# Batch 0's keys in five whole pieces, fewer dummy products, and a new order of every queue

## The chip, the cores and the metric
One core of a Trainium2 chip runs the whole program. It has TensorE (PE, matrix products), VectorE (DVE), ScalarE (ACT), GpSimd (POOL) and SyncE (SP, which only issues transfers), each with a queue of its own that it works through in order. The metric is the time on the device in microseconds (us); lower is better.

## The reference, cut to what matters
Three stages in float32 follow one another: attention over 2 batches, 8 heads, 768 positions and 64 values a head; a gated network with two weight matrices of 512x1024 and a gate of 512x512; and a mixer over positions and channels.

```python
k_sum = k.reshape(B, H, nb, 32, D).max(axis=3)          # block maxima of the keys
v_sum = v.reshape(B, H, nb, 32, D).mean(axis=3)
scores_l = where(|i - j| < 16, scale * q @ k.T, -1e9)    # a window of near keys
scores_s = scale * q @ k_sum.T + log(32)                # and all 24 block maxima
x = softmax(concat(scores_l, scores_s)) @ concat(v, v_sum)
x = sigmoid(xr @ w_r) * (relu(xk @ w_k) ** 2 @ w_v)      # xk, xr: x mixed with its row before
u = x + (relu(x.T @ w_tok1) @ w_tok2).T
out = u + relu(u @ w_ch1) @ w_ch2
```

The weights come as float64 and are turned on the chip into two float32 parts, so each weight product is made of three.

## The kernel before, in words
A batch's queries are cut into 6 tiles of 128 positions. For a tile, the key tile `kw` holds 160 keys (the window) and, in front and behind, 24 columns for the block maxima. Every score row needs the maxima of all blocks, so no score can be made before all of the batch's keys have been seen. For batch 0 `k_load` (L484) brings six key tiles of 128x4x160 by SP and ScalarE's queue in turn, `k_max` (L489) takes the maxima of a tile on VectorE into `ks`, and `kw_sums` (L497) copies `ks` into the two places of a tile on GpSimd.

For one tile and one of the two heads of a pair ("unit"; 12 in batch 0) `s_stage` (L563) makes scores on TensorE (`sp<-kw,xT`), VectorE adds the mask and takes the row minimum of the negated score (`pe`, `mn`), ScalarE takes the exponential and its sum (`pe`, `dens`). TensorE transposes (`pt`), the result is copied (`PT`), and TensorE multiplies it with values (`pv`). `rb` spreads one over the sums over the array, and VectorE multiplies it in (`xT<-xT,rb`). `vt_sum` (L512) adds up v's blocks on VectorE (`vrs`), two rows of 768 elements in one instruction, and `vp` transposes these sums. `q_load` (L555) brings q of batch 0 into a part of `xT` that is free then.

As soon as two tiles of x are there, the weight products of the second stage start: `ko` (with w_k, in groups of two blocks of 128 columns) and `acc` (with w_v). A weight tile (`wst`, 512 KB) is turned into two parts by ScalarE, VectorE, ScalarE (`w<-wf`) and GpSimd in turn. The products are laid between the attention's.

Dummy products, `spin` (L826), whose result nothing reads, run on TensorE: eight of 512 columns at the start, one more of that width after each of the first eight units' scores, and `paced` (L833): one of 256 columns for each key tile but the first, which reads `ks` and so comes behind that tile's maxima.

The order on every engine is written out by hand in `PLANS` (L57), a list of tile names with counts; `keep` (L231) ties each instruction to the one before it in the list. So an engine never works ahead of an instruction that waits. SP's list is the order in which transfers are issued; at most eight of them are on the way at a time.

Of the kernel before, what the change touches and what calls it, by code (L numbers as in the profile page):

```python
# [14 lines left out]
ALU = mybir.AluOpType  # L15
# [16 lines left out]
SPIN0, PACED = 8, 1  # L32
# [26 lines left out]
        spin*12 sp*16 spin sp*24 spin pt*4 sp*8 spin vp pt vp spin pt vp*2 pt*2 spin pt*4 sp*8 rb*8 pt spin pt  # L59
        pv*16 pt sp*8 pt spin pv*16 pt*4 rb*8 sp*8 pt*2 pt@24 pt@22*2 pt@25*2 pv*16 pt sp*8 rb*8 sp*16 pt*4 pv*8  # L60
        pt*3 pv*8 pt spin rb*8 ko pt*2 ko*7 pt@40 ko*3 pt@38 ko*10 pt@41 ko*3 spin ko*2 pt@39 ko*2 pt@42 ko pt
        ko pv*8 rb*8 ko*2 pv*8 acc ko*10 pv*8 acc ko*3 acc ko*3 vp*2 sp*16 acc ko*2 pt ko*2 pt*2 acc ko pt ko
        acc*4 acc@12 acc@9*2 ko*2 vp pv*8 acc rb*8 ko*5 acc@13 acc@15 ko*3 acc*2 ko*4 acc@21 acc@14 ko*4 acc@18
        ko*2 acc acc@22 vp acc@20 sp*16 ko*3 acc@24 ko acc@23 ko*2 acc@27*3 ko acc@33 acc@25*2 sp*16 acc@30 ko
        pt acc pt ko acc acc@34 pt ko*3 acc ko*4 pt*2 ko*3 pt ko pt@56 pt@54 sp ko pt ko pt@57 sp*15 pt pv*16 pt
        ko*3 pt ko*17 pt ko*2 pt ko acc pt acc ko pt*3 acc@39 pv*16 ko pt acc ko acc@38 ko acc@42 ko acc@41
        acc@43 ko acc ko*4 pt acc*3 ko*7 acc pt ko*4 acc ko acc@51*2 pt ko acc@50 ko pt ko acc@54*2 acc@53
        acc@57 ko*9 acc@56 ko*2 pv*16 ko*5 acc@58 ko acc ko acc*2 acc@63 pt ko*2 acc ko*3 acc@62 ko pt sp*3
        acc@66 acc@65 acc@67 pt*2 acc ko*10 acc@72 ko*2 pt ko*8 pt acc@69*2 ko*2 acc acc@73 ko*2 acc acc@78
        acc@75*3 ko acc@81 pt ko acc acc@79 ko*9 acc@83 pt acc@87 ko*8 pv*16 ko acc@80 acc@88*2 acc@84 ko*4  # L70
# [12 lines left out]
        ro*2 acc ro@21 ko ro acc@211 ko ro acc@215 ko*2 acc@212 ko acc@219 ko*10 acc@216*2 ko acc@220 ko*6 ro ko
        acc@218 ro acc@221*2 ro ko acc@225 ro@36*3 ro@27 acc*2 ro@39*3 ro@28 ro@42 ro@29 acc@223*2 ro ro@43
        acc@231 ro@31*4 acc@228 ro@44 ro@35 acc ro@45*2 ko*2 ro ko*7 acc ko*8 acc@234 acc@232*2 ko*7 ro acc@237
        ro@60 acc acc@235 ko*2 acc@239 ko*3 ro@49 ko ro acc@236 ro*3 ko ro*3 ko ro ro@61 h1 ko ro ro@58 ko*3 ro
        ko*7 acc@240 ko*5 ro@63 acc*2 acc@246 ro acc@243*3 ko*5 ro acc@247 acc@249*2 acc@248 acc@251 acc@255
        ro*4 ko*3 ro ko ro ko*6 acc@252 acc@256 ko*2 ro acc@253 ko acc@257 ko h1 ko*5 ro*2 acc@254 acc@258*2
        ro*2 ko*3 acc ro acc*2 ko*4 ro*3 ko ro ko h1 ro ko*7 h1@18 ko ro@84 ko*3 h1@3 acc ko ro ko*2 ro acc@267
        h1 ro acc@264 acc@268*2 acc@265 ro ko acc ro@83 acc@273 ro@89*2 h1@19 acc@270 ro*3 acc@274 h1 acc@271 ro  # L90
        h1@5*2 ro h1*2 acc@275 h1 acc@272 acc@276*2 h1 acc@279 h1 acc acc@278 acc@282 acc@281 acc@283 h1 acc@285
        h1 acc h1@21*2 acc@284 acc@287 h1@14 ro h1 ro@108 h1*2 ro@97*2 ro@109 h1@23*2 ro@99 ro@110 h1*2 ho@12
        ro@100*2 h1*2 ro@111 ro@102 h1 ro*4 ro@112*3 h1*6 ho*2 ro@107 ro@115*2 ho*2 ro*3 ho*2 ho@21 ho@19 ho@22
        ho@20 ro ho@23 ro@132 ro@121 ro@133 ro@122*4 ro@134*4 ro@126*2 ro@138*4 h1 ro*2 h1*2 ro@128*4 h1*8
# [1270 lines left out]
```

## Time and profile before

| | |
|---|---|
| time, median of 3 runs | 494.56 us (493.72 to 495.25) |
| the profiled execution's own time | 495.46 us |
| its span, first to last instruction | 493.7 us |
| TensorE busy | 482.9 us (98%), 3290 products |
| VectorE busy | 293.4 us (59%) |
| ScalarE busy | 248.1 us (50%) |
| GpSimd busy | 210.3 us (43%) |
| transfers | 70.63 MB, mean 143 GB/s |

Busy time of TensorE counts each product to the end of its pipeline, so a busy TensorE can still have small waits between products, and dummy products count as busy. A product in plain float32 stands in the trace as two products. An engine's share over the whole span says little here: VectorE is busy for 59% of the span, and much more than that in the first 64 us. The granted clock in the rows (PEclk) is a share of full speed.

### The profile page before, as it was taken

How to read it: one execution, taken by the hardware profiler on the slowest of the kernel's cores; microseconds unless marked ns; L12 is line 12 of the kernel's file. 1: busy time of each engine (PE TensorE's matmuls, PEld its weight loads, DVE VectorE, ACT ScalarE, POOL GpSimd, SP SyncE). 2: the span in 40 equal slices, each digit the busy share in tenths (PEclk: the TensorE clock that was granted, in tenths of full speed). 3: DMA queues.
4: the chain of work that ended last, by engine and by line, in shares of the span. 5: the costliest groups of instructions: out<-in, count | busy, mean ns of one | idle time of the engine just before them, and what ended most of it. 6: DMA issues, size and time to landing. Idle time of an engine off the chain costs nothing.

```text
span 493.7 us, 8740 instructions
## 1 busy us (share of the span) xinstructions
PE 482.9 (98%) x3290; PEld 403.3 (82%) x3290; DVE 293.4 (59%) x638; ACT 248.1 (50%) x569; POOL 210.3 (43%) x266
## 2 busy tenths in 40 slices
PE   8999999999999999999999999999999999999996
PEld 3678787888898888888888767787898888988884
DVE  3699996544543243757777788268395537354253
ACT  1698758763545663575876542554543323111110
POOL 5246577864545224263455333858815501100000
PEclk9999999999999999999999999999999999999998
DMA  9999961340200520002646746828860405061402
GB/s 271 336 319 345 339 206 21 118 134 21 61 1 2 193 105 1 0 1 53 208 158 224 253 102 214 293 83 250 271 241 20 149 27 187 18 219 42 150 1 85
DMA packets 35914, 70.63 MB, mean 143 GB/s; under 512 B 3072, under 2 KB 12288, under 8 KB 35872
## 3 DMA queue, kind: packets, MB, share of 16 engines
q1 hardware_dynamic: 34288, 69.09, 43.7%
q10 hardware_dynamic: 1584, 0.98, 0.6%
q8 instruction: 26, 0.43, 0.4%
q14 instruction: 16, 0.13, 0.1%
HBM read 60.04 MB, written 9.44 MB: 141 GB/s over the span
## 4 chain that ended last, share of the span: by engine, by line
PE 84%; DVE 7%; issue 3%; POOL 3%; ACT 2%; DMA 1%; DVEq 0%; POOLq 0%; SPq 0%; ACTq 0%
PE o L225 16%; PE ko L225 14%; PE acc L225 14%; PE m L225 9%; PE ro L225 7%; PE go L225 5%; PE spin L225 4%; PE sp L225 3%; PE pv L225 3%; PE h L225 3%; PE pt L225 2%; DVE wf L225 2%; POOL w L225 2%; PE ho L225 1%; DVE ybuf L225 1%
## 5 line engine op out<-in xcount | busy, mean ns | idle before, releaser
L225 PE MATMUL o<-w,gh 128*128 128x512 f32 x288 | 100.7, 399 | 0.3 <-ACT gh L225 0.2
L225 POOL TENSOR_TENSOR w<-wf,w 128x512 fp32r<-128x512 f32 x50 | 69.6, 1399 | 53.9 <-ACT w L225 53.7
L225 PE MATMUL m<-u,w 128*128 128x256 f32 x504 | 85.7, 282 | 0.9 <-ACT f L225 0.7
L225 PE MATMUL ko<-xh,w 128*128 128x256 f32 x384 | 84.8, 288 | 0.6 <-ACT rl L225 0.5
L225 PEld LDWEIGHTS m<-u,w 128*128 128x128 f32 x504 | 77.4, 189 | 8.9 <-ACT f L225 1.2
L225 PEld LDWEIGHTS ko<-xh,w 128*128 128x128 f32 x384 | 65.2, 188 | 7.5 <-ACT rl L225 1.3
L225 PE MATMUL acc<-w,kh 128*128 128x512 f32 x192 | 68.4, 403 | 0.0
L225 PEld LDWEIGHTS o<-w,gh 128*128 128x128 f32 x288 | 52.3, 188 | 9.3 <-ACT gh L225 1.7
L225 POOL TENSOR_TENSOR kl<-rl,kh 128x512 fp32r<-128x512 f32 x24 | 31.5, 1314 | 58.7 <-ACT kh L225 42.5
L225 PE MATMUL o<-w,gl 128*128 128x512 f32 x144 | 54.7, 395 | 0.0
L225 PE MATMUL ko<-xl,w 128*128 128x256 f32 x192 | 54.6, 285 | 0.0
L225 PE MATMUL go<-u,w 128*128 128x512 f32 x144 | 45.4, 400 | 0.1
L225 ACT ACTIVATE wst<-wst 128x512 f32<-128x512 f32 x62 | 40.2, 670 | 8.5 <-DMA wst<-in_moe_w_ch_dram 8.5
L225 ACT ACTIVATE pe<-pe,mn 128x120 f32<-128x120 f32 x96 | 37.0, 387 | 14.7 <-DVE mn L225 14.1
L225 DVE SCALAR_TENSOR_TENSOR xk<-xT,mus,tmp 128x256 f32<-128x256 f32 x52 | 31.0, 613 | 16.0 <-ACT tmp L225 12.4
L225 ACT CAST w<-wf 128x512 fp32r<-128x512 f32 x50 | 30.4, 616 | 19.8 <-DVE wf L225 17.5
L225 ACT ACTIVATE gh<-m 128x512 fp32r<-128x512 f32 x24 | 14.2, 598 | 51.2 <-DVE m L225 51.2
L225 DVE SCALAR_TENSOR_TENSOR wf<-wst,wf 128x512 int32<-128x512 int32 x50 | 36.5, 735 | 3.6 <-ACT wst L225 2.5
L225 PEld LDWEIGHTS acc<-w,kh 128*128 128x128 f32 x192 | 34.2, 188 | 5.1 <-issue 0.5
L225 PEld LDWEIGHTS ko<-xl,w 128*128 128x128 f32 x192 | 36.1, 188 | 2.4 <-issue 0.2
L225 PE MATMUL acc<-w,kl 128*128 128x512 f32 x96 | 37.8, 400 | 0.0
L225 DVE TENSOR_SCALAR wf<-wst 128x512 int32<-128x512 int32 x50 | 28.2, 568 | 15.2 <-POOL w L225 15.2
(111 smaller groups left out, 897.5 us busy)
## 6 DMA issues: line engine op xcount, KB each, us to landing
wst<-in_moe_w_ch_dram SPq DMA_DIRECT2D x36, 512.0 KB
w<-stored SPq DMA_DIRECT2D x24, 512.0 KB
stored<-w SPq DMA_DIRECT2D x24, 256.0 KB
wst<-in_moe_w_k_dram SPq DMA_DIRECT2D x8, 512.0 KB
wst<-in_moe_w_v_dram SPq DMA_DIRECT2D x8, 512.0 KB
wst<-in_moe_w_tok_dram SPq DMA_DIRECT2D x6, 512.0 KB
out_dram<-o SPq DMA_DIRECT2D x12, 256.0 KB
kw<-in_k_dram SPq DMA_DIRECT2D x9, 320.0 KB
```

Of the source, the lines that this page charges most:

```text
L225: inst = fn(*args, **kw)
```

## The change
Batch 0's keys come as a tensor of their own, `ka`, laid out by pair of heads, in pieces of 128x800 (the last cut into 416 and 384 columns), on SP alone. They land in `kall`, the end of `ybuf`, which later holds values and results. The maxima are taken from there, a piece at a time, and each key tile is copied on the chip from `kall`: tiles 0 to 3 on ScalarE (tile 0 in two halves), tiles 4 and 5 on GpSimd. q of batch 0 is stored so that each row of it is one stretch in `xT`. v's sums of batch 0 are four instructions instead of two. ScalarE gets a first exponential of one column, so that its table is loaded at once. The paced products are gone; six dummies of 512 columns stand at the start, and the units' dummies have 256. All five lists in `PLANS` are new, from start to end.

```diff
-SPIN0, PACED = 8, 1
+SPIN0 = 6
+KA = 4
@@ PLANS: all five lists
...
+    warm = const.tile([128, 1], F32, name="warm")
+    nc.scalar.activation(warm, ident[:, 0:1], AF.Exp)
...
     def k_load(b, t):
-        q = nc.scalar if b == 0 and t % 2 else nc.sync
-        after(q.dma_start(kw[:, :, K0:K0 + 2 * HALF], k[b, t]))
+        after(nc.sync.dma_start(kw[:, :, K0:K0 + 2 * HALF], k[b - 1, t]))
+    NKA = NP * (S + 2 * WINDOW)
+    kall = ybuf.rearrange("p a n -> p (a n)")[:, B * NT * DM - NKA:].rearrange("p (a s) -> p a s", a=NP)
+    def halves(p):
+        return ((0, S // 2), (S // 2, S)) if p == NP - 1 else ((0, S),)
+    def keys_load(p):
+        for i, j in halves(p):
+            i, j = i and i + 2 * WINDOW, j + 2 * WINDOW
+            nc.sync.dma_start(kall[:, p, i:j], ka[p][:, i:j])
+    def keys_max(p):
+        for i, j in halves(p):
+            x = kall[:, p, WINDOW + i:WINDOW + j].rearrange("p (n w) -> p n w", w=BLOCK)
+            nc.vector.tensor_reduce(st_of(0)["ks"][:, p, i // BLOCK:j // BLOCK], x, AX.X, ALU.max)
+    def keys_copy(t):
+        kw = st_of(0)["kw"][t] = at.tile([128, NP, WC], F32, tag="kw", bufs=KB, name="kw")
+        for ps in (slice(0, 2), slice(2, NP)) if t == 0 else (slice(0, NP),):
+            dst, src = kw[:, ps, K0:K0 + 2 * HALF], kall[:, ps, 128 * t:128 * t + 2 * HALF]
+            if t < KA:
+                nc.scalar.copy(dst, src)
+            else:
+                nc.gpsimd.tensor_scalar(dst, src, 1.0, 1.0, ALU.mult, ALU.mult)
...
     def vt_sum(b, j):
-        r = nc.vector.tensor_reduce(st["vr"][:, 2 * j:2 * j + 2], st.pop(("vt", j)), AX.X, ALU.add)
-        if b == 0:
-            behind(r, lows[-1:])
+        x = st.pop(("vt", j))
+        for c in range(2) if b == 0 else (slice(0, 2),):
+            r = nc.vector.tensor_reduce(st["vr"][:, 2 * j:2 * j + 2][:, c], x[:, c], AX.X, ALU.add)
...
     def attention():
-                    spin(SPIN)
+                    spin(SPIN, 2)
...
-    def spin(n):
+    def spin(n, w=4):
...
-            after(nc.tensor.matmul(o, ident, ident.unsqueeze(1).to_broadcast([128, 4, 128]), start=True, stop=True))
-    def paced(t):
...
+            after(nc.tensor.matmul(o[:, :w], ident, ident.unsqueeze(1).to_broadcast([128, w, 128]), start=True, stop=True))
     spin(SPIN0)
+    for p in range(NP):
+        keys_load(p)
+    for p in range(NP):
+        keys_max(p)
     for t in range(NT):
-        k_load(0, t)
+        keys_copy(t)
```

TensorE's list at its start, before: the first dummies, the paced products (`spin<-ks`), the first scores.

```order
L225 MATMUL spin<-ident 128x512 x8
L225 MATMUL spin<-ks,ident 128x256 x4
L225 MATMUL sp<-kw,xT 64x120 x16
L225 MATMUL spin<-ks,ident 128x256
L225 MATMUL sp<-kw,xT 64x120 x24
L225 MATMUL spin<-ident 128x512
L225 MATMUL pt<-ident,pe 120x128 x4
L225 MATMUL sp<-kw,xT 64x120 x8
```

The same place after the change:

```order
L235 MATMUL spin<-ident 128x512 x6
L235 MATMUL spin<-ident 128x256 x2
L235 MATMUL sp<-kw,xT 64x120 x16
L235 MATMUL spin<-ident 128x256
L235 MATMUL pt<-ident,pe 120x128
L235 MATMUL sp<-kw,xT 64x120 x16
L235 MATMUL spin<-ident 128x256 x2
L235 MATMUL vp<-ident,vrs 24x128
L235 MATMUL pt<-ident,pe 120x128 x3
L235 MATMUL vp<-ident,vrs 24x128 x3
L235 MATMUL sp<-kw,xT 64x120 x16
```

No product reads `ks` any more; two of the units' dummies stand ahead of the first score, and the transposes of v's sums come earlier among the scores.

SP's list at its start, before (`xT<-in_q` and `xT<-in_vt` are q and v for the sums, `wst` the weights, `ybuf<-in_v` the values):

```order
L225 DMA kw<-in_k_dram 128x4x160 x3
L225 DMA xT<-in_q_dram 128x4x128 x3
L225 DMA xT<-in_vt_dram 128x2x768 x2
L225 DMA ybuf<-in_v_dram 96x512
L225 DMA wst<-in_moe_w_k_dram 128x512
L225 DMA wst<-in_moe_w_v_dram 128x512
L225 DMA xT<-in_q_dram 128x4x128
```

And after:

```order
L235 DMA ybuf<-in_ka_dram 128x800 x3
L235 DMA ybuf<-in_ka_dram 128x416
L235 DMA ybuf<-in_ka_dram 128x384
L235 DMA xT<-in_q_dram 128x512 x2
L235 DMA mus<-in_mu_dram 128x8
L235 DMA xT<-in_vt_dram 128x2x768 x2
L235 DMA wst<-in_moe_w_v_dram 128x512
L235 DMA xT<-in_q_dram 128x512
L235 DMA ybuf<-in_v_dram 96x512
```

The five pieces of keys stand first, then two tiles of q; the other three key tiles that ScalarE's queue issued are gone from there.

SP's list further on, before: from the third w_k tile (`wst_147`) to batch 1's key tiles (`kw`).

```order
L225 DMA wst_147<-in_moe_w_k_dram 128x512
L225 DMA wst_155<-in_moe_w_v_dram 128x512
L225 DMA wst_149<-in_moe_w_v_dram 128x512
L225 DMA wst_153<-in_moe_w_k_dram 128x512
L225 DMA kw_625<-in_k_dram 128x4x160
L225 DMA wst_157<-in_moe_w_k_dram 128x512
L225 DMA ybuf_71<-in_v_dram 96x512
L225 DMA kw_810<-in_k_dram 128x4x160
L225 DMA wst_161<-in_moe_w_k_dram 128x512
```

And after, from batch 1's first key tile to the sixth w_k tile (`wst_170`):

```order
L235 DMA kw_461<-in_k_dram 128x4x160
L235 DMA kw_624<-in_k_dram 128x4x160
L235 DMA wst_166<-in_moe_w_k_dram 128x512
L235 DMA kw_809<-in_k_dram 128x4x160
L235 DMA ybuf_73<-in_v_dram 96x512
L235 DMA kw_1013<-in_k_dram 128x4x160
L235 DMA kw_1121<-in_k_dram 128x4x160
L235 DMA wst_168<-in_moe_w_v_dram 128x512
L235 DMA kw_1123<-in_k_dram 128x4x160
L235 DMA ybuf_73<-in_vt_dram 128x1536
L235 DMA qT_922<-in_q_dram 128x512
L235 DMA wst_170<-in_moe_w_k_dram 128x512
```

All six key tiles of batch 1 and its first v for the sums now stand ahead of the sixth w_k tile.

## Rows read from the trace of the kernel before

**Rows 1.** Busy us (count) by stage, all engines; then clock, transfer share, GB/s

```profile
14.00:36.00 22.00, 21.26 (x245) 15.29 (x245) 19.04 (x85) 18.37 (x75) 6.79 (x14) 1.00 1.07 318
36.00:50.00 14.00, 14.00 (x188) 11.24 (x188) 12.73 (x48) 12.48 (x35) 8.63 (x8) 1.00 1.05 347
50.00:64.00 14.00, 13.26 (x133) 11.26 (x130) 12.98 (x27) 10.28 (x30) 9.02 (x9) 1.00 1.06 353
...
120.00:200.00 80.00, 80.00 (x617) 70.39 (x616) 32.54 (x85) 42.10 (x97) 32.07 (x42) 1.00 0.17 57
```

**Rows 2.** TensorE in order of time: start, us, what, count, idle before

```profile
1.46 9.58 PE L225 MATMUL spin<-ident 128*128 128x512 f32 x16 [1.46 <-POOL ident masks.py:199]
11.10 2.97 PE L225 MATMUL spin<-ks,ident 128*128 128x256 f32 x8
14.00 1.51 PE L225 MATMUL sp<-kw,xT 64*64 64x120 f32 x32
15.44 0.70 PE L225 MATMUL spin<-ks,ident 128*128 128x256 f32 x2
16.32 1.78 PE L225 MATMUL sp<-kw,xT 64*64 64x120 f32 x32 [0.18 <-issue]
...
19.36 1.12 PE L225 MATMUL spin<-ident 128*128 128x512 f32 x2
...
32.34 1.02 PE L225 MATMUL spin<-ident 128*128 128x512 f32 x2
...
48.70 1.02 PE L225 MATMUL spin<-ident 128*128 128x512 f32 x2
...
50.68 0.39 PE L225 MATMUL ko<-xh,w 128*128 128x256 f32 x1
```

**Rows 3.** VectorE in order of time: maxima of the keys, first scores

```profile
5.00 0.69 DVE L225 TENSOR_REDUCE ks<-kw 128x16 f32<-128x512 f32 x1 [5.00 <-DMA kw<-in_k_dram]
...
8.90 1.28 DVE L225 TENSOR_REDUCE ks<-kw 128x16 f32<-128x512 f32 x2 [0.35 <-DMA kw<-in_k_dram]
15.21 0.28 DVE L225 CUSTOM_DVE_ANT_0 pe<-sp,mask 128x120 f32<-128x120 f32 x1 [5.03 <-PE sp L225]
```

**Rows 4.** GpSimd in order of time: maxima into tiles, first value sums

```profile
10.27 0.74 POOL L225 TENSOR_SCALAR kw<-ks 128x96 f32<-128x96 f32 x3 [4.52 <-DVE ks L225]
...
25.15 1.71 POOL L225 COPY ybuf<-vs 24x512 f32<-24x512 f32 x3 [9.87 <-ACT vs L225]
```

**Rows 5.** The chain that ended last, shares of the span by engine

```profile
PE 84%; DVE 7%; issue 3%; POOL 3%; ACT 2%; DMA 1%; DVEq 0%; POOLq 0%; SPq 0%; ACTq 0%
```

**Rows 6.** Dummy products alone by stretch: PE busy (count), PEld, clock, transfers

```profile
1.40:5.90 4.50, 4.44 (x6) 1.87 (x7) 1.00 0.88 263
...
6.60:10.90 4.30, 4.30 (x11) 1.70 (x9) 1.00 1.18 317
```

**Rows 7.** Busy by stretch again; read the last column, GB/s

```profile
2.00:3.00 1.00, 1.00 (x2) 0.34 (x1) 0.00 (x0) 0.00 (x0) 0.90 (x6) 1.00 0.76 185
...
25.00:62.00 37.00, 35.99 (x422) 28.69 (x421) 33.86 (x106) 31.51 (x97) 21.41 (x24) 1.00 1.07 334
```

**Rows 8.** VectorE's groups to 64 us: shape, count, busy us, mean ns

```profile
L225 DVE TENSOR_REDUCE ks<-kw 128x16 f32<-128x512 f32 x12 | 7.7, 678 | 6.3 <-DMA kw<-in_k_dram 6.3
...
L225 DVE TENSOR_REDUCE vrs<-xT 128x48 f32<-128x1536 f32 x2 | 3.4, 1744 | 0.0
```

**Rows 9.** ScalarE's groups from 14 to 64 us, idle before them last

```profile
L225 ACT ACTIVATE wst<-wst 128x512 f32<-128x512 f32 x13 | 8.6, 676 | 0.0
...
L225 ACT COPY xT<-pv 128x512 f32<-128x512 f32 x5 | 2.9, 583 | 0.0
...
L225 ACT CAST xh<-xk 128x1024 fp32r<-128x1024 f32 x1 | 1.0, 1043 | 0.0
```

**Rows 10.** GpSimd's groups from 14 to 64 us

```profile
L225 POOL TENSOR_SCALAR tmp<-xT,oms 128x256 f32<-128x256 f32 x8 | 5.8, 730 | 4.8 <-DVE xT L225 2.6 <-DVE xk L225 1.8 <-POOL w L225 0.4
```

**Rows 11.** ScalarE in order of time: its first exponential

```profile
16.14 0.39 ACT L225 ACTIVATE pe<-pe,mn 128x120 f32<-128x120 f32 x1 [11.82 <-DVE mn L225]
```

More of the change, by code (lines that the diff above doesn't have):

```diff
@@ new lines @@
+        xk@41 xk@43 ybuf y wf xl xk rl xk*3 ybuf y xl wf*4 ybuf wf xk h xk wf@60 wf@59 xk*2 wf@61 xl ybuf h ybuf
+        wf wf@64*2 y@4 y@3 ybuf@20 ybuf@19 wf@63 wf@66 ybuf@15 wf*2 ybuf wf y@5 ybuf*2 wf*3 gl wf*3 u ybuf@21*2
+        gl wf*2 u wf ybuf wf@80 wf@79 wf@81 ybuf f4 u ybuf u wf wf@84*2 ybuf wf@83 ybuf gl f4@2 ybuf gl wf@86
+        wf@88 wf@87 wf@89 f4@4 f4@1 f4@5*2 wf*2 f4@3 sum gl*2 f4@7 sum gl*2 wf*2 f4 f4@10 wf wf@96 wf@95 wf@97
+        f4 gl wf f4 wf f4 f4@9 sum gl f4@14 gl f4 sum gl sum@5 sum@4 gl sum@6*3 gl u u@6 sum o sum f4@18 u@5 sum
@@ new lines @@
+        kw@20*2 pe pe@11 pe@9*2 pe@15 pe@13 pe@12 pe@16 pe@14 w@13 pe@18 pe@17 pe@19 kl w@15 pe kw@23 kw@22 tmp
+        kl tmp pe*2 kl pe*2 tmp pe@31 tmp kw@24 pe@29 pe@25 kw tmp pe@28 kl pe@30 tmp pe@26*2 pe@32 pe@37 kl tmp
+        pe@36 tmp kl pe@39 tmp*2 pe@33 w@17 pe@38 pe@34 kl pe@43 pe@42 pe@35 kl*2 tmp*2 pe@40*2 kl w@16 pe@45
+        pe@44 pe@47 pe@46 kl*2 w@18 kl*2 w kl tmp w w@22 tmp w@21 kl tmp*2 kl w@24 y kl*2 w w@23 kl w@26 y kl y
+        w*3 y w y w@32 w@31 y w@34 w@33 w@35*6 w@42 w@41 w@43*3 sum w@47 sum w*2 sum w@46 w@51 w@50 sum w@52*4
@@ L258, in fused_kernel @@
 @with_exitstack
-def fused_kernel(ctx, tc, q, k, v, vt, mu, w_k, w_v, w_r, w_t1, w_t2, w_c1, w_c2, out):
+def fused_kernel(ctx, tc, q, ka, k, v, vt, mu, w_k, w_v, w_r, w_t1, w_t2, w_c1, w_c2, out):
     nc = Queues(tc.nc)
@@ L556, in q_load @@
         if b == 0:
-            st_of(b)["qT"][t] = xT[:, :, XB + 1 + 128 * t:XB + 129 + 128 * t]
-        else:
-            st_of(b)["qT"][t] = at.tile([128, NP, 128], F32, tag="qT", bufs=QB, name="qT")
-        after(nc.sync.dma_start(st_of(b)["qT"][t], q[b, t]))
+            if t < KD:
+                dst, src = xT[:, t, XB + 1:XB + 513], q[b, t].rearrange("p a n -> p (a n)")
+                st_of(b)["qT"][t] = [dst[:, 128 * p:128 * p + 128] for p in range(NP)]
+            else:
+                z = 2 * (t - KD)
+                dst = [xT[:, z + i, XB + 513:XB + 769] for i in range(2)]
+                st_of(b)["qT"][t] = [dst[p // 2][:, p % 2 * 128:p % 2 * 128 + 128] for p in range(NP)]
+                for i in range(2):
+                    after(nc.sync.dma_start(dst[i], q[b, t][:, 2 * i:2 * i + 2].rearrange("p c n -> p (c n)")))
+                return
+        else:
+            dst, src = at.tile([128, NP, 128], F32, tag="qT", bufs=QB, name="qT"), q[b, t]
+            st_of(b)["qT"][t] = [dst[:, p] for p in range(NP)]
+        after(nc.sync.dma_start(dst, src))
     @ahead(HS)
@@ L573, in s_stage @@
                     r = slice(64 * e, 64 * e + 64)
-                    m = nc.tensor.matmul(sp[64 * half:64 * half + 64, p], qT[r, p, 64 * half:64 * half + 64],
+                    m = nc.tensor.matmul(sp[64 * half:64 * half + 64, p], qT[p][r, 64 * half:64 * half + 64],
                                          kw[r, p, c0:c0 + NC], start=True, stop=True)
@@ L877, in fused_kernel @@
         masks.append(mc)
-    for t in range(NT):
-        ahead(HK)(k_max)(0, t)
-        if t >= PACED:
-            paced(t)
     kw_sums(0, 0)
@@ L1336, in laid_out @@
         "q": by_values(q).reshape(B, 2 * D, H // 2, nt, 128).transpose(0, 3, 1, 2, 4),
-        "k": np.stack([kp[..., 128 * t:128 * t + 128 + 2 * WINDOW] for t in range(nt)], axis=1),
+        "ka": kp[0].transpose(1, 0, 2),
+        "k": np.stack([kp[1:, ..., 128 * t:128 * t + 128 + 2 * WINDOW] for t in range(nt)], axis=1),
         "v": np.pad(v, pad).transpose(0, 2, 1, 3).reshape(B, S + 2 * WINDOW, H * D),
```

295 lines of the change are left out of this document (146 added, 149 removed).

## The prediction, made before the changed kernel ran

> **What bounds the kernel now.** I read the busy time by stage first, then TensorE's rows in order of time, then those of VectorE and GpSimd, and last the chain that ended last. From 120 to 200 us TensorE is busy all of the time [rows 1], and in the whole chain it holds 84% [rows 5]: once the weights are there the rest runs as fast as products can be issued. So a microsecond is lost where TensorE does something that the result does not need, and that is the front. Until 14.00 it runs only dummy products: sixteen halves of the eight wide ones (an fp32 product shows as two rows) from 1.46 on, and then four that read `ks`, 2.97 us, ahead of the first score [rows 2]. A fifth follows at 15.44, and the next score starts at 16.32. After that eight more wide dummies stand among the scores, from 19.36 on; the first useful weight product (`ko`) is at 50.68 [rows 2].
>
> What does the first score need? Keys, their block maxima, q. VectorE takes its last two maxima at 8.90 and ends at 10.18 [rows 3]; GpSimd copies the maxima into the key tiles from 10.27, three in 0.74 [rows 4], so the two for tile 0 are there by 10.8. The score stands at 14.00 because of the order on TensorE: the paced products are ahead of it.
>
> Between 14 and 64 three engines are nearly full: VectorE is busy 19.04 of 22, 12.73 of 14 and 12.98 of 14 us, ScalarE 18.37, 12.48 and 10.28 [rows 1]. VectorE's first work on a score is at 15.21 [rows 3], so it has 48.8 us to 64, is busy 44.75 and idle 4.0. This is the engine that limits what can be won behind the first score.
>
> **The change part by part.** *Dummies ahead of the first score.* TensorE has six wide ones now and then two of half width (unit dummies moved forward), no paced ones. Of the sixteen halves, six start before 5.9; the other ten fill 6.6 to 10.9, 0.43 each [rows 6]. Twelve halves therefore end at 10.9 - 4 x 0.43 = 9.2, and four halves of half width at 0.215 add 0.9: TensorE is free for the first score at about 10.0, against 14.00. Worth 4.0, if the data is there.
>
> *Keys.* Six tiles of 128x4x160 (1.97 MB) on two queues become five pieces (1.64 MB) on SP's queue. Bytes flow from about 2.4 us (185 GB/s in the slice from 2 to 3); with SP alone issuing, 25 to 62 us, it is 334 GB/s [rows 7]. 1.64 MB is then in by about 7.4; taking instead the 8.90 at which the last tiles land now [rows 3] and subtracting the 0.33 MB saved (1.0 us) gives 7.9, which I take, being the measured row; without any saving it is 8.9. VectorE's maxima by row length: 678 ns for 512 elements, 1744 for 1536, so 1.04 ns per element and 0.15 fixed [rows 8]; the last half piece (384) costs 0.5 and the earlier ones lie under the transfers. Two copies on GpSimd follow at 0.25 each with 0.1 of handover [rows 4]: ready at 9.1, at worst 10.1. ScalarE's copies into tile 0 need only the first four pieces and are done before. q of tile 0 is next behind the keys (0.26 MB, 0.8 us): 8.7. So the dummies set the first score, not the keys: 10.0, at worst 11.0 with a late landing.
>
> *The fifth paced product and the unit dummies.* The paced one goes: 16.32 - 15.44 = 0.9. Eight wide dummies (2 x 0.43 each) become six of half width behind the first score: 6.9 - 2.6 = 4.3. Together 5.2 us of TensorE's time, worth 0 if VectorE and ScalarE cannot deliver sooner, all of it if they can.
>
> *v's sums in four rows.* Two of 1744 ns become four of 768 elements: 0.15 + 0.80 = 0.95 each, 3.8 against 3.5, a cost of 0.3 on VectorE, which has no cover there. What it buys is that masks of the next scores go between.
>
> *Copies.* On ScalarE a copy is 583 ns for 512 and 1043 for 1024 elements [rows 9], so 0.70 for 640. Three (two half ones) stand ahead of its first exponential, in time that it idles now: 11.82 us before 16.14 [rows 11]. Two, 1.4 us, stand among the first exponentials, and the transposes wait behind them; to 64 us ScalarE has 6.8 us idle (47.9 less 41.1), so I cost them at nothing, 1.4 if that cover is gone. On GpSimd 730 ns for 256 elements [rows 10] makes 1.8 for each of two copies, in the 9.87 us that it idles before 25.15 [rows 4]. The first stands ahead of tile 1's second copy of the maxima: about 12.6 instead of 10. TensorE comes there behind a transpose that needs the first exponential, 2.1 us after the first score (16.14 less 14.00), so at 12.2 to 12.6: nothing to 0.5.
>
> *The table load* lies at 3 us in an idle stretch now: nothing. *SP's new order:* 0.33 MB less in a stream that is full to 62 us [rows 7]; the later w_k tiles stand behind batch 1's six key tiles. ScalarE never waited on a landing for its 13 weight steps up to 64 (idle before them 0.0) [rows 9], so I cost it at nothing; a rival below prices it.
>
> **The sum.** 4.0 is sure if the order holds. Of the 5.2, VectorE's slack allows at most 4.0 - 0.3 = 3.7; an engine fed by three others does not lose all its idle time, and I take about half, 1.7. Gain 5.7 (from 2.5, with keys late and the copies uncovered, to 9.2). The profiled execution took 495.46 (span 493.7 and 1.8 around it): 489.8. The runs' median, 494.56, lies 0.9 lower: **488.9**.
>
> **One rule weighed.** Wide dummies took 0.85 each half until about 6 us and 0.43 after [rows 6]: 1.2 and 2.4 GHz, although the granted clock reads 1.00 in both. From 33.3 to 48.70 no dummy stands at all, only scores, transposes, value and reciprocal products, and the dummy at 48.70 (two halves in 1.02 with the last one's tail) still runs at the high level [rows 2]. The Trainium skill, TensorE: Matmul & The Clock Gate (Part 1 and Part 4), says that the array falls to half its clock when idle and that PE-mode transposes do not count as busy in the same way. By that rule fewer and narrower dummies could cost the clock; by the row they do not.
>
> **Rivals.**
> 1. *TensorE gets all its time back* (chance 0.12). For it: its rows stand end to end from 14 to 50. Against: VectorE's 92%. Gain 9.2: 485.4.
> 2. *Weights come late* (0.12). Adding up the sizes on SP's queue, the sixth w_k tile had 13.3 MB issued up to and with it, now 15.5; at 334 GB/s it lands 6.6 us later, about 49, while its products (the third group of `ko`) come some 5 us earlier, by my count of the products ahead of them at 54 to 58. After a landing come ScalarE, VectorE, GpSimd steps of some 4 us, so it is close. If products wait 3 to 4 us there, the gain is about 2: 492.5.
> 3. *Copies in front of the exponentials bind* (0.08). ScalarE paces the front: 4.0 less 1.4 less 0.3: 492.3.
> 4. *Slower: the clock falls* (0.07) in the stretch from the first score to the first weight product, by the halved dummies. Work there then takes double. The gain is eaten when 5.7 us of work runs at 1.2 GHz; with 12 us of it so, 494.56 + 12 - 5.7 = 501. Against it stands the stretch without dummies.
> 5. *The start does not move* (0.03): keys through one queue land as late as 12 or later; 494.5.
>
> The forecast has the remaining 0.58. This kernel tells 0.3% (1.5 us) from no change. Faster: 0.58 + 0.12 + most of 2 and 3 (0.16) = 0.86; same: 0.03 + 0.04 = 0.07; slower 0.07. Range from rival 1 to rivals 2 and 3 with room for a late start: 485.3 to 493.0.
>
> **What would show it.** First score at 9.5 to 10.5 right behind a dummy, not behind a wait for keys; the last maximum on VectorE ending by 8.5; first exponential near 12.1; first `ko` between 39 and 45; a weight step of ScalarE that idles for a landing would speak for rival 2; dummy halves of half width at 0.43 instead of 0.215 behind 12 us for rival 4. TensorE full from 120 on as before. Wrong: a first score after 11.5, or a first `ko` as late as 48.

## The result, and the profile after

The changed kernel takes 482.68 us (median of 4 runs, 482.37 to 483.38), the kernel before in the same comparison 494.73: a ratio of 0.976, interval 0.974 to 0.978. That is 12.05 us faster; 5.7 was forecast (488.9), and the time lies below the range of 485.3 to 493.0. The profiled execution's span is 480.7 us.

TensorE in order of time (start, us, what, count), to be held against [rows 2]:

```profile
1.46 8.80 PE L235 MATMUL spin<-ident 128*128 128x512 f32 x16 [1.46 <-POOL ident masks.py:199]
10.19 1.51 PE L235 MATMUL sp<-kw,xT 64*64 64x120 f32 x32
11.63 0.70 PE L235 MATMUL spin<-ident 128*128 128x256 f32 x2
...
14.23 1.46 PE L235 MATMUL spin<-ident 128*128 128x256 f32 x4
...
21.64 1.15 PE L235 MATMUL pv<-PT,ybuf 120*64 120x64 f32 x16
...
41.76 0.36 PE L235 MATMUL ko<-xh,w 128*128 128x256 f32 x1
```

The row of sixteen holds twelve halves of 512 columns and four of 256. The first score stands right behind a dummy at 10.19 (before 14.00), and the first `ko` at 41.76 (before 50.68): 8.9 of the 12 us are there by then, 5.1 of them behind the first score.

VectorE in order of time, to be held against [rows 3, 8]:

```profile
6.53 1.87 DVE L235 TENSOR_REDUCE ks<-ybuf 128x24 f32<-128x768 f32 x3 [0.63 <-DMA ybuf<-in_ka_dram]
11.40 0.28 DVE L235 CUSTOM_DVE_ANT_0 pe<-sp,mask 128x120 f32<-128x120 f32 x1 [3.00 <-PE sp L235]
...
13.03 1.81 DVE L235 TENSOR_REDUCE vrs<-xT 128x24 f32<-128x768 f32 x2
...
14.96 0.95 DVE L235 TENSOR_REDUCE vrs<-xT 128x24 f32<-128x768 f32 x1
...
16.02 0.95 DVE L235 TENSOR_REDUCE vrs<-xT 128x24 f32<-128x768 f32 x1
```

The maxima end at 8.40. What the forecast passed over is below them: v's sums come 1.6 behind the first mask (13.03 less 11.40). In the kernel before they came 3.8 behind it (15.21, [rows 3]), with 16 masks ahead of them:

```profile
19.02 3.41 DVE L225 TENSOR_REDUCE vrs<-xT 128x48 f32<-128x1536 f32 x2
```

GpSimd, and then ScalarE, at the copies (against [rows 4, 10] and [rows 9, 11]):

```profile
8.49 0.51 POOL L235 TENSOR_SCALAR kw<-ks 128x96 f32<-128x96 f32 x2 [2.42 <-DVE ks L235]
...
9.69 0.72 POOL L235 TENSOR_SCALAR kw<-ybuf 128x640 f32<-128x640 f32 x1
```

```profile
11.73 0.39 ACT L235 ACTIVATE pe<-pe,mn 128x120 f32<-128x120 f32 x1 [3.51 <-DVE mn L235]
...
12.12 0.71 ACT L235 COPY kw<-ybuf 128x640 f32<-128x640 f32 x1
```

Busy time by stage: the two windows that answer to [rows 1], and two late ones, of the changed kernel and then of the kernel before:

```profile
10.20:32.00 21.80, 20.32 (x270) 16.03 (x271) 19.88 (x91) 19.23 (x69) 11.37 (x27) 1.00 1.06 299
32.00:60.00 28.00, 27.94 (x328) 23.59 (x323) 25.33 (x80) 23.57 (x73) 16.55 (x22) 1.00 1.06 338
...
250.00:290.00 40.00, 40.00 (x186) 32.20 (x185) 33.54 (x56) 24.43 (x44) 19.68 (x15) 1.00 0.62 207
350.00:400.00 50.00, 50.00 (x332) 45.49 (x331) 30.51 (x49) 17.76 (x34) 17.23 (x15) 1.00 0.31 98
```

```profile
260.00:300.00 40.00, 38.76 (x179) 30.65 (x178) 31.77 (x54) 21.84 (x39) 16.50 (x14) 1.00 0.67 211
360.00:410.00 50.00, 48.89 (x320) 43.59 (x320) 28.05 (x48) 16.28 (x31) 16.26 (x14) 1.00 0.35 118
```

VectorE was hardly fuller in the front than before (19.88 of 21.80, then 25.33 of 28), and TensorE moves faster. Late in the program the kernel before was not full: in these windows TensorE lacks 1.24 of 40 and 1.11 of 50 us, and nothing in the changed kernel. The forecast had looked at 120 to 200 alone. In the chain that ended last TensorE now holds 92%, where [rows 5] had 84%.

**A lead for each microsecond of work.** To say where time is won I let every useful product count its usual spacing (a dummy counts nothing; 444.3 us in all), and note when each kernel has issued so much of it. This is worked out from the trace's starts. The lead over the kernel before's profiled run, in us (negative: earlier), with the kernels of the next section:

```
us of useful work      5     15     65    125    185    245    285    365    425
changed kernel      -1.3   -6.8   -8.9   -9.8   -8.6   -8.6  -10.3  -12.8  -12.4
b_nodum             -1.4   -0.2   -0.4   -0.4   -0.4   -0.4   -1.0   -1.0   -1.0
a_none              -1.2   -3.9   -7.0   -7.9   -6.6   -6.6   -8.3  -10.8  -10.4
a_front_old         -2.7   -0.2   -0.2   -0.3   +0.9   +0.9   -0.9   -3.4   -2.9
b_front_new          0.0   -6.2   -8.4   -9.0   -8.9   -8.9   -9.3   -9.2   -9.2
b_early_new         +0.5   -2.7   -2.9   -3.0   -2.9   -2.9   -4.1   -4.0   -4.0
b_all_new            0.0   -6.2   -8.4   -9.1   -7.9   -7.9   -9.6  -12.1  -12.0
a_late_old          -0.5   -5.9   -8.2   -9.1   -7.8   -5.9   -7.4   -7.3   -7.1
b_late_new           0.0    0.0    0.0    0.0    0.0   +2.9   +1.2   -1.4   -1.2
a_mid_old           -1.3   -6.8   -8.9   -9.7   -9.8   -6.3   -8.0  -10.5  -10.1
a_vlate             +3.6   +0.3   -1.8   -2.7   -1.5   -1.5   -3.2   -5.7   -5.2
a_table             -0.8   -6.3   -8.5   -9.4   -9.3   -9.2  -11.0  -13.5  -13.0
```

The changed kernel wins 9.8 up to 125 us, gives back 1.2 near 160, and wins 4 more behind 245. The columns at 5 and 15 depend on what is taken as the usual spacing: with each kind's median they move by up to 4 us, the others by less than 1.5. So those two are read only roughly.

### The profile page after: what moved, and what is told of

Read it like the earlier page. It is cut to its first block, busy times and chain, and to the rows that moved or that the text cites. A ratio compares the mean times of both kernels' runs of the same rounds, so it can differ in the third digit from the quotient of the medians.

```text
span 480.7 us, 8744 instructions
## 1 busy us (share of the span) xinstructions
PE 472.2 (98%) x3276; PEld 400.7 (83%) x3276; DVE 287.6 (60%) x639; ACT 252.3 (52%) x575; POOL 215.3 (45%) x268
## 4 chain that ended last, share of the span: by engine, by line
PE 92%; DVE 5%; ACT 1%; issue 1%; POOL 0%; DVEq 0%; ACTq 0%; POOLq 0%
PE o L235 20%; PE ko L235 14%; PE acc L235 14%; PE m L235 13%; PE ro L235 7%; PE go L235 6%; PE h L235 3%; PE ho L235 3%; PE pv L235 3%; PE sp L235 2%; PE spin L235 2%; PE pt L235 2%; DVE wf L235 1%; PE rb L235 1%; DVE pe L235 1%; PE utr L235 1%
## 5 line engine op out<-in xcount | busy, mean ns | idle before, releaser
L235 PE MATMUL m<-u,w 128*128 128x256 f32 x504 | 90.7, 284 | 0.0
L235 PE MATMUL ko<-xh,w 128*128 128x256 f32 x384 | 88.1, 287 | 0.1
L235 PEld LDWEIGHTS m<-u,w 128*128 128x128 f32 x504 | 79.9, 189 | 7.1 <-DVE mw L235 0.2
L235 PEld LDWEIGHTS ko<-xh,w 128*128 128x128 f32 x384 | 67.0, 188 | 7.9 <-ACT rl L235 1.5
L235 PE MATMUL acc<-w,kh 128*128 128x512 f32 x192 | 70.4, 402 | 0.0
L235 POOL TENSOR_TENSOR kl<-rl,kh 128x512 fp32r<-128x512 f32 x24 | 33.7, 1405 | 51.3 <-ACT kh L235 32.9
L235 PE MATMUL go<-u,w 128*128 128x512 f32 x144 | 46.6, 399 | 0.0
L235 DVE SCALAR_TENSOR_TENSOR xk<-xT,mus,tmp 128x256 f32<-128x256 f32 x52 | 27.1, 537 | 16.7 <-ACT tmp L235 12.8
L235 PE MATMUL ro<-w,xh 128*128 128x512 f32 x96 | 34.2, 395 | 0.9 <-ACT xh L235 0.9
```

The costliest lines, as they stand in the source:

```text
L235: inst = fn(*args, **kw)
```

## The experiments

Labels with `b_` are the kernel before with an edit, those with `a_` the changed kernel. Where only the order differs, the lists are cut at a time of each kernel's own trace at which both have begun nearly the same work; what has begun by then keeps its order, the rest takes the other kernel's. Times are medians; a ratio stands to the kernel before, timed beside it.

### Do the dummies limit the front?

**b_nopaced**

```diff
     for t in range(NT):
         ahead(HK)(k_max)(0, t)
-        if t >= PACED:
-            paced(t)
@@ "tensor"
-        spin*12 sp*16 spin sp*24 spin pt*4
+        spin*8 sp*40 spin pt*4
```

> The kernel before without its five paced products, nothing else. Theory 1 (TensorE itself is what limits the front, and every microsecond taken out of its list there comes back at the end): the first score comes 3.0 earlier, at 11.0, the fifth product gives its 0.88 too; -3.9, about 490.8. Theory 2 (that of the prediction: VectorE's slack limits what is won behind the first score): -3.0 for the start and 0.3 of the fifth, about 491.4.

494.74 us, ratio 1.002 (0.998 to 1.006): nothing won. TensorE in order of time:

```profile
12.21 1.74 PE L216 MATMUL sp<-kw,xT 64*64 64x120 f32 x32 [1.90 <-DMA xT<-in_q_dram]
14.75 4.39 PE L216 MATMUL sp<-kw,xT 64*64 64x120 f32 x48 [0.80 <-POOL kw L216]
```

With the dummies gone a wait for q, 1.90 us, stands in their place, and 48 rows of scores take 4.39 us, where 32 took 1.78 [rows 2]: the granted clock reads 0.56 from 14.70 to 19.10. Both theories missed this. So the run does not show what the five products would be worth with the clock held.

**b_nodum**

```diff
-SPIN, SPIN_UNITS = 1, 8
+SPIN, SPIN_UNITS = 1, 0
@@ "tensor": no `spin` but the first eight; and the edit of b_nopaced
```

> The kernel before without the paced products and without the eight units' dummies (0.86 to 0.97 each from start to the next product, 7.4 together); only the eight at the start stay. Theory 1: -3.9 - 7.4 = -11.3, about 483.4. Theory 2: -3.0 for the start and at most half of the 8.3 us that VectorE's slack leaves, 1.7: about 490. Rival (the clock needs the dummies): the first scores run at half the clock, 490 to 500, with transposes and scores twice as long in the trace.

493.37 us, 0.998 (0.996 to 1.000). Some 11 us of dummies are gone, and 1.2 us of time, at the edge of what these runs tell apart. TensorE:

```profile
23.22 1.06 PE L215 MATMUL pt<-ident,pe 128*120 128x128 f32 x4 [1.49 <-ACT vs L215]
24.21 1.87 PE L215 MATMUL sp<-kw,xT 64*64 64x120 f32 x16
...
28.52 1.75 PE L215 MATMUL pv<-PT,ybuf 120*64 120x64 f32 x15
```

The same places in the kernel before, and then the busy time of this run in the stretch between them:

```profile
25.38 0.60 PE L225 MATMUL pt<-ident,pe 128*120 128x128 f32 x4
...
29.13 1.90 PE L225 MATMUL pv<-PT,ybuf 120*64 120x64 f32 x32
```

```profile
24.00:30.00 6.00, 6.00 (x51) 4.82 (x51) 4.82 (x15) 4.59 (x18) 1.45 (x3) 0.50 1.08 292
```

The transposes wait for ScalarE's copy of v's sums (`vs`) and come 2.2 earlier than before, where some 7.4 us of dummies had stood ahead of them: most of these had filled waits. Then the granted clock is 0.50, transposes and scores take nearly twice as long, and the first value product is only 0.6 earlier. So the rival with the clock came too, and 1.6 of the 2.2 are lost while it is low. Theory 1 is out, since 2.2 is far from 7.4 even before the clock falls; theory 2 had expected 4.5 in all.

**a_none**

```diff
-SPIN, SPIN_UNITS = 1, 8
+SPIN, SPIN_UNITS = 1, 0
@@ "tensor"
-        spin*8 sp*16 spin pt sp*16 spin*2 vp
+        spin*6 sp*16 pt sp*16 vp
```

> The changed kernel without the units' dummies; six wide ones at the start stay. Two of the eight stand ahead of the first score: it comes at 9.1 behind the copies of the maxima, instead of 10.19, -1.1. The other six take 4.3 from their start to the next product. Theory 1: -5.4, about 477.3. Theory 2: -1.1 and at most 0.7 more, about 481. Rival (the clock needs them): above 482.7, with products at twice their duration between 9 and 40 us.

484.77 us, 0.980 (0.979 to 0.982): 2.1 slower than the changed kernel. TensorE, and then busy time by stage (the clock is the third number from the right):

```profile
15.29 0.39 PE L227 MATMUL vp<-ident,vrs 128*24 128x128 f32 x1 [1.66 <-DVE vrs L227]
...
17.10 2.73 PE L227 MATMUL sp<-kw,xT 64*64 64x120 f32 x32
```

```profile
13.80:27.40 13.60, 12.07 (x97) 9.56 (x99) 11.08 (x50) 9.86 (x40) 4.10 (x9) 0.50 1.05 307
```

A wait of 1.66 for v's sums stands where two dummies were, and from 13.80, early in that wait, to 27.40 the clock is at 0.50, its lower level of 1.2 GHz. The rival of the expectation came: without the dummies the clock falls, and with some 5 us of them gone the kernel is slower.

### Is it the order, or keys, sums and dummies?

**a_front_old**

```diff
@@ PLANS, all five lists
-    the changed order
+    up to 160.2 us of the kernel before: its order; then the changed one
```

> The changed kernel (its keys, v's sums row by row, its dummies), but with all five lists in the order of the kernel before up to 160 us of that kernel's time, and the changed order behind it. Taking out dummies alone gained 0 and 1.2, so they are not what the front gained. Theory F (the new order of the queues in the front gives what was won behind the first score, some 5 us of 8.7): the first score stays near 10.2, but the first ko comes at 46 or later instead of 41.8, and the time is about 487.5. Theory K (the earlier keys, with TensorE less laden, carry the front): at most 484.

491.79 us, 0.993 (0.991 to 0.996). TensorE:

```profile
9.34 1.74 PE L224 MATMUL sp<-kw,xT 64*64 64x120 f32 x32 [0.61 <-POOL kw L224]
11.98 2.72 PE L224 MATMUL sp<-kw,xT 64*64 64x120 f32 x32 [0.91 <-POOL kw L224]
...
28.70 1.49 PE L224 MATMUL pv<-PT,ybuf 120*64 120x64 f32 x25
```

VectorE's sums of v, and then busy time:

```profile
15.57 3.53 DVE L224 TENSOR_REDUCE vrs<-xT 128x24 f32<-128x768 f32 x4
```

```profile
12.10:25.60 13.50, 13.17 (x87) 10.39 (x88) 9.01 (x47) 10.17 (x40) 3.77 (x14) 0.50 0.86 227
```

The first score is 4.7 earlier than before, v's sums end 3.3 earlier (19.10 against 22.43), and the first value product is 0.4 earlier; by 15 us of work the lead is 0.2. Waits of 0.61 and 0.91 come in, and the granted clock is 0.50 from 12.10 to 25.60, with TensorE busy nearly all of that time. So what theory K hoped for did not come, but the time is 4.3 above what theory F expected: in the old order the changed dummies lose the clock, and most of the early start is lost while it is low. This run alone does not part the order from the clock; the next two, at a clock of 1.00, show whether the keys are needed.

**b_front_new**

```diff
-SPIN0, PACED = 8, 1
+SPIN0, PACED = 6, 6
-                    spin(SPIN)
+                    spin(SPIN, 2)
@@ PLANS, all five lists
+    up to 149.6 us of the changed kernel: its order; then the old one
```

> The kernel before (its six key tiles, v's sums two rows at a time) with the changed kernel's dummies and the changed order on all queues up to 150 us of the changed kernel's time, the old order behind. First score at 12.2 to 12.4, since keys and then q land no earlier than in the runs without dummies. Theory F: -1.7 at the start and some 5 behind it, about 488. Theory K: 492.5 to 494.

487.53 us, 0.986 (0.982 to 0.990). The first score is at 11.08, but the lead at 5 us of work is still 0.0, and yet the lead is 6.2 at 15 us and 8.9 at 185. Theory F holds, and theory K, which had expected 492.5 to 494, is out.

**b_all_new**

```diff
@@ as b_front_new, and
@@ PLANS, all five lists
+    the changed order from start to end
```

> The kernel before (its key tiles loaded from memory, v's sums two rows at a time) with the changed kernel's dummies and the changed order of all five queues from start to end. Theory F (orders carry nearly all of the gain): 483 to 484, at most 1 slower than the changed kernel, although its first score comes near 11 to 12. Theory K (the keys on the chip and the sums row by row are needed): 486 or more.

482.71 us, 0.976 (0.974 to 0.979): the changed kernel's time, with key tiles from memory, no copies on the chip, v's sums two rows at a time, and the table load where it was. Its first score is at 11.09, 0.9 later than in the changed kernel, and its span is 480.9 against 480.7: most of that later start is made up. Fewer dummies in the old order are worth 1.2 at most (b_nodum), so the new order is what the 12 us need; the keys, the copies and the split sums are not. The new order with the old dummies was not run, so what order and dummies are worth apart is not shown.

**b_early_new**

```diff
@@ as b_front_new, but
+    up to 21.6 us of the changed kernel: its order; then the old one
```

> As b_front_new, but the changed order only for what the changed kernel started in its first 21.6 us (up to its first value product), the old order behind. In b_front_new TensorE's lead over the kernel before was 6.2 us by then and 9.0 at 85 us of work. If what counts is the early order (v's sums behind 8 masks instead of 16, one unit's exponentials at a time): 488 to 489. If the order behind is needed to keep it: above 491.

494.12 us, 0.999 (0.997 to 1.002); its profiled run, 491.54, was the fastest of twelve. The lead is 2.7 at 15 us, about 3 up to 245 and 4 behind that; v's sums reach ScalarE at 19.28 (b_all_new: 18.79), but the first value product is at 26.66 against 22.19. TensorE:

```profile
25.27 1.09 PE L216 MATMUL rb<-ident,dens 128*64 128x128 f32 x16 [2.14 <-DVE PT L216]
```

As expected for that case, the early order alone does not keep its lead. But 2.14 of it go in this wait for VectorE's copy (`PT`), 3.7 behind the place where the orders meet, so a cost of the cut and the worth of the order behind it are not parted here.

### Which place of the order?

**a_vlate**

```diff
@@ "vector"
-        ks*5 pe*8 vrs@3 vrs@2 pe vrs@0 pe vrs pe*4 dens pe*2 dens
+        ks*5 pe*14 dens pe*2 vrs@3 vrs@2 vrs@0 vrs dens
```

> The changed kernel with one thing in VectorE's list put back: the four instructions of v's sums behind 16 masks, as in the kernel before, not behind 8, 9 and 10. If the place of v's sums is what made the front early (TensorE's order has their transposes ahead of all value products): the first value product comes 2 to 5 later than 21.64, and the time is 2 to 4 longer, 485 to 487. If the place of the sums alone does little: within 1 of 482.7.

489.47 us, 0.988 (0.987 to 0.989): four instructions put back, with all other lists as changed, cost 6.8 us. TensorE, then busy time:

```profile
20.27 0.28 PE L227 MATMUL vp<-ident,vrs 128*24 128x128 f32 x1 [3.68 <-DVE vrs L227]
...
21.87 2.73 PE L227 MATMUL sp<-kw,xT 64*64 64x120 f32 x32
```

```profile
20.20:31.00 10.80, 10.49 (x84) 8.13 (x85) 7.13 (x31) 5.34 (x19) 3.22 (x5) 0.53 1.06 265
```

TensorE waits 3.68 for the sums, since their transposes stand ahead of everything else on its list, and then the clock is 0.53 over eleven microseconds. That is more than was expected, because the price is paid twice: the wait, and the clock behind it.

**a_vrs2**

```diff
-        for c in range(2) if b == 0 else (slice(0, 2),):
+        for c in (slice(0, 2),):
@@ "vector"
-        pe*8 vrs@3 vrs@2 pe vrs@0 pe vrs
+        pe*8 vrs@1 pe vrs@0
```

> The changed kernel with v's sums in two instructions of two rows each, the first behind 8 masks, the second behind 9. The forecast gave the split a cost of 0.3 on VectorE. By the trace of the old program in the new order the split is worth at most the 1.0 that TensorE waits for the sums there. Expected 482.4 to 483.7; equal to the changed kernel if neither matters.

502.72 us, 1.015 (1.013 to 1.018): far outside what was expected. One of its six executions took 1608 us; nothing on record says why. VectorE:

```profile
30.39 1.75 DVE L227 TENSOR_REDUCE vrs<-xT 128x48 f32<-128x1536 f32 x1 [16.20 <-DMA xT<-in_q_dram]
```

By the profile a sum over two rows waits 16.2 us for a landing of q in `xT`; sums of one row do not, and in b_all_new (q laid out as before) two rows don't either. So the split is no matter of VectorE's time. It seems to keep the sums apart from q's new places; which overlap makes the wait was not tried.

**a_spin5**

```diff
-SPIN0 = 6
+SPIN0 = 5
```

> The changed kernel with five wide dummies at the start instead of six. One takes 0.86: the first score comes at 9.33 if the maxima (in place at 9.0) allow it. If in the new order the first score sets the chain: -0.85, 481.8. If it does not (in the old order 2.5 us of start were lost at once): 482.7. If the gap or fewer products cost the clock: slower.

482.16 us, 0.974 (0.972 to 0.976), not to be told from the changed kernel. The first score is at 10.33, not 9.33: in this profile dummy halves took 0.85 until 6.7, in the changed kernel's only until 5.0, so the clock rose later and the test of an earlier start did not come about.

### The back, and the sigmoid's table

**a_late_old**

```diff
@@ PLANS, all five lists
+    behind 257.5 us of the changed kernel: the order of the kernel before
```

> The changed kernel up to 257.5 us of its own time; what stands in its five lists behind that is put in the order of the kernel before. Theory A (the new orders late in the program give the last 4 us of the gain): 4 us slower than the changed kernel, 486.7, with TensorE waiting between 265 and 290 and between 365 and 400. Theory B (the late gain follows from the earlier start, since weights and buffers have more time): as the changed kernel, 482.7.

488.48 us, 0.987 (0.984 to 0.989). Busy time of the stages shown above:

```profile
257.00:297.00 40.00, 38.43 (x177) 30.13 (x176) 33.17 (x53) 20.66 (x37) 16.21 (x13) 1.00 0.60 194
355.00:405.00 50.00, 48.92 (x315) 43.37 (x314) 27.49 (x48) 16.12 (x32) 15.99 (x15) 1.00 0.32 111
```

With the early front kept the time is 5.8 above the changed kernel. All of what TensorE lacks in the first window is a wait of 1.57 at 261, where the orders meet: a cost of the cut. The gap of the kernel before (1.19, ahead of `ho` at 289.48) did not come back; the second gap did. Theory A's 4 fits what is left. Without such a wait at the cut, b_front_new and b_all_new, which differ in the order behind 149.6 us alone, are 4.8 apart (3.5 in their profiled spans).

**b_late_new**

```diff
@@ PLANS, all five lists
+    behind 265.8 us of the kernel before: the changed order
```

> The kernel before up to 265.8 us of its own time; what stands in its five lists behind that is put in the changed order. Theory A (the late orders are worth what the changed kernel lost when it got the old ones, 4.5 to 5.8): 489 to 490. Theory B (the new late order needs the earlier front): 494.5.

494.29 us, 0.999 (0.998 to 1.000): theory A's time is missed, and theory B's met. But the lead table shows that the late order still wins: 2.9 are lost where the orders meet (a wait of 2.44 for ScalarE's `y` that ends at 270.71), and 4.3 won from there to 365.

**a_mid_old**

```diff
@@ PLANS, all five lists
+    from 149.6 to 257.5 us of the changed kernel: the order of the kernel before
```

> The changed kernel with the old order between 149.6 and 257.5 us only. There the changed kernel gave back 1.2 of what it had won (its lead over the kernel before falls from 9.9 to 8.6 near 190 us). If the order does that: 481.5; if the place where the two orders meet costs something or the loss has another cause: 482.7 or above.

485.81 us, 0.982 (0.979 to 0.985). The 1.2 is kept (lead 9.8 at 185, not 8.6), but the second cut costs a wait of 3.05 for `y`:

```profile
261.48 0.50 PE L224 MATMUL h<-y,w 128*128 128x512 f32 x1 [3.05 <-ACT y L224]
```

So the changed order does lose 1.2 near 185; this row of the changed kernel and ScalarE's rows beside it show where:

```profile
185.06 0.50 PE L235 MATMUL ro<-w,xh 128*128 128x512 f32 x1 [0.86 <-ACT xh L235]
```

```profile
182.18 1.28 ACT L235 ACT_TABLE_LOAD   x1
183.48 0.58 ACT L235 ACTIVATE ro<-ro 128x512 f32<-128x512 f32 x1
183.97 1.04 ACT L235 CAST xh<-xk 128x1024 fp32r<-128x1024 f32 x1
```

**a_xh**

```diff
@@ "scalar"
-        rl w@21 ro xh kh ro
+        rl w@21 xh ro kh ro
```

> The changed kernel with one pair exchanged in ScalarE's list: the cast xh of the last group of the second batch stands ahead of the first sigmoid (which brings its table load, 1.28, with it). In the changed kernel the cast ended 1.0 after TensorE had come to it: 0.86 of idle time before ro at 185.06, and products at a slower pace around it. If that wait is all of what was given back there (1.2): 481.5. If the next wait is right behind: 482.2 to 482.7.

486.11 us, 0.981 (0.979 to 0.983): slower. TensorE, then busy time:

```profile
187.34 0.50 PE L227 MATMUL ro<-w,xh 128*128 128x512 f32 x1 [2.35 <-DVE ybuf L227]
```

```profile
188.00:190.00 2.00, 2.00 (x9) 1.71 (x8) 2.00 (x4) 0.00 (x0) 1.56 (x1) 0.50 0.00 0
```

The profile names the cast as what ended the wait at 185.06; but `ro` also needs the bank that the sigmoid works on and that VectorE then reads (`ybuf`), and the sigmoid stood behind the table load. Moved back further, it made TensorE wait 2.35, and the clock fell to 0.50 behind it.

**a_table**

```diff
     nc.scalar.activation(warm, ident[:, 0:1], AF.Exp)
+    nc.scalar.activation(warm, ident[:, 0:1], AF.Sigmoid)
@@ "scalar"
-        wst@21 wst@23 w w@22 rl w@21 ro xh
+        wst@21 wst@23 w warm w@22 rl w@21 ro xh
```

> The changed kernel with a sigmoid of one column in ScalarE's list 3 us earlier, where it idles before 179.49, so that the table is loaded there and not in front of the first sigmoid of the gate. The exchanged cast made things worse because TensorE's next ro waits for the sigmoid to empty its bank (idle 2.35 there, 0.86 in the changed kernel). If the table load (1.28) is the cause of the 1.2 given back near 185: 481.4 to 481.8, no idle time before ro at 185. If another wait is right behind: 482.7.

481.93 us, 0.973 (0.971 to 0.974): the lowest of all, some 0.7 below the changed kernel, and 0.1 above what was expected. The difference is small: its five executions (481.05 to 482.36) lie just under the changed kernel's four (482.37 to 483.38). No idle time is left before `ro`, and the lead is 9.3 at 185. The load stands where ScalarE idled:

```profile
176.84 1.28 ACT L227 ACT_TABLE_LOAD   x1
178.13 0.20 ACT L227 ACTIVATE warm<-ident 128x1 f32<-128x1 f32 x1
179.97 0.62 ACT L227 CAST w<-wf 128x512 fp32r<-128x512 f32 x1 [1.63 <-DVE wf L227]
```

That casts and `rl` run on behind it without another load agrees with the Trainium skill, ScalarE: Activation LUTs (Table sets: the hidden batching unit): cheap functions such as relu and copy are in every set.

## Why the prediction was wrong

**The step that failed** is the one that had no term: the new order of the five lists. SP's got a sentence ("so I cost it at nothing"), the others none, though the change says that all of them are new from start to end. The old program with the new order and its fewer dummies gains 12 us (b_all_new), with the fewer dummies alone 1.2 (b_nodum). In the new program the old order in the front takes 9 back, part of it by the clock (a_front_old), and the old order late some 4 (a_late_old, without the 1.57 where the orders meet).

**The first score: "4.0 is sure if the order holds".** The time was right (10.0; 10.19) and the maxima too (8.4), its worth was not. In the old order a first score 4.7 earlier gave 0.4 at the first value product, with 2.9 lost behind v's sums while the clock was low (a_front_old). In the new order a first score 0.9 later went with 0.2 at the end (b_all_new). Nor did it wait for dummies alone: without them, with q as before, it waited for q until 12.21 (b_nopaced). The next thing late was v's sums, 16 masks behind the first mask (19.02 less 15.21) and 3.4 long; the trace held both numbers, and the forecast did not follow the chain from them to the first value product.

**The 5.2 of dummies.** Mis-sized: a half of 256 columns takes 0.32 from its start to that of the second half, not 0.215, so some 4.3 were freed; the forecast's own row of eight such halves in 2.97 us [rows 2] says 0.37. And mis-read: rows end to end on TensorE [rows 2] looked like a full engine, but most of the dummies were laid into waits. Taking them out is worth 0 to 1.2 in the old order and -2.1 in the new one, in each case with the clock's fall in it.

**"VectorE's slack allows at most 4.0 - 0.3 = 3.7"** was no limit: 5.1 were won behind the first score by 41.76. Four of its instructions in another place, with the same work, cost 6.8 (a_vlate). A busy share says how much an engine does, not whether it does first what the others wait for.

**v's sums in four rows, 0.3**: the size was right (3.7 to 3.8 against 3.4 to 3.5); that the split keeps a wait for q away (a_vrs2) was not seen. **Copies at nothing**: right; ScalarE's 0.71 as forecast, GpSimd's 0.72 and not 1.8, since 730 ns for 256 elements [rows 10] was another kind of operation. **The table load at the start at nothing**: right (b_all_new has it in its old place); the one for the sigmoid at 182, which it did not look at, is worth some 0.7 (a_table).

**"TensorE full from 120 on as before"**: full in the changed kernel, not before, as two windows of the trace would have told. There the order won 4. Its idle time explains 2.35 of that; the rest is wider spacing between products, with no single cause found.

**The rivals.** Rival 1 named 9.2, near what the front gave, by a wrong mechanism. Rivals 2, 3 and 5 did not come. Rival 4, the clock, did not come in the changed kernel (1.00) and came where TensorE was left to wait in the front: 0.56 (b_nopaced), 0.50 (b_nodum, a_none, a_front_old), 0.53 (a_vlate). Its sign, halves of half width at 0.43 instead of 0.215, could not have told it: they take 0.32 at a clock of 1.00. The argument against it, that no dummies stand from 33 to 48.7 and the clock holds, was taken from a stretch almost without waits (the longest 0.26). The Trainium skill, TensorE: Matmul & The Clock Gate (Part 1), says that the array falls to half its clock when it idles. The front's runs agree with the direction; the wait of 3.05 us at 261 (a_mid_old), after which the clock stays at 1.00, shows that not every wait does it.

**Open:** a_vlate settles one place of the front's order. Which other entries carry the rest (b_early_new loses 5 to 6 of 9 with the order of the first 21.6 us alone) was not taken apart. Nor was the order parted from the number of dummies, or the clock's part in the runs with the old order from the order's own.

## What to carry to other kernels

When a change brings a new order of the queues, price that first: follow one item from the first input to the first use of its result on every list, in both orders, and only then count what is removed. Filler on a full engine may stand in a wait; before crediting its removal, find what would be waited for then, and whether the clock survives the wait. And read every stage for idle time, not the one in the middle.

## What the runs showed of the hardware

After a wait of 1.49 us (b_nodum, to 23.22), 0.91 us (a_front_old, to 11.98) or 2.35 us (a_xh, to 187.34) on TensorE the granted clock was 0.50, for at least 6, 13 and 2 us. In a_none it fell early in a wait of 1.66 us, behind one of 0.57. But it stayed at 1.00 after waits of 2.14 us (b_early_new, to 25.27), 2.44 us (b_late_new, to 270.71) and 3.05 us (a_mid_old, to 261.48). So the length of the last wait does not tell by itself whether the clock falls. When it rose at the start differed between executions: dummy halves fell from 0.85 to 0.43 at 5.0, 5.9 or 6.7 us in three profiles with the same dummies up to there.
